# Recurrent attention and a two-layer network on one core: eight chunks of load buffers, later stores, two more chunks turned by DMA

## The chip, the core and the metric

The kernel runs on one core of one Trainium2 chip. A core has five engines with instruction streams of their own: TensorE (PE, matrix products), VectorE (DVE), ScalarE (ACT), GpSimd (POOL) and SyncE (SP). Data moves between main memory and on-chip memory on 16 DMA engines; here SP issues loads and DMA transposes, and POOL issues most stores. The metric is the device time of one execution in microseconds (us), the median of three runs.

## The reference

Four sequences of 768 steps, with 8 heads of 48 numbers, go through a linear recurrence with a decay (step 1). The result, 3072 rows of 384 numbers, goes through two matrix products with a squared relu between them (step 2).

```python
# q, k, v, alpha: (4, 8, 768, 48); alpha lies between 0.8 and 1
for t in range(768):
    state = alpha[:, :, t, :, None] * state + einsum('bhd,bhe->bhde', k[:, :, t], v[:, :, t])
    y[:, :, t] = einsum('bhd,bhde->bhe', q[:, :, t], state)
x = y.transpose(0, 2, 1, 3).reshape(3072, 384)
out = (maximum(x @ w_in, 0) ** 2) @ w_out        # w_in 384x2048, w_out 2048x384
```

## The kernel before

**Chunks.** The 3072 rows are 24 chunks of 128 steps, six to a sequence. Chunks 0 to 3 are handled as two double chunks (`add_super`); chunks 4 to 23 one by one (`add_chunk`), with the scores and what follows them in pairs from chunk 8 on.

**Step 1 in one chunk.** The four inputs of a chunk are loaded by SP (`add_load`, line 362; 192 KB each) into buffers that hold two chunks each, three per input, so six chunks. ACT takes the logarithm of alpha (L431); PE sums it over the steps with a triangle of ones; ACT makes A and its inverse (L459, L463) by exponentials; DVE multiplies q by A (L490, from chunk 12 on) and k by the inverse (L493). POOL casts v (L436). From chunk 12 on A's last row, the chunk's total decay, is sent to where it is needed by two small DMAs that POOL issues (`e_aed`, L476). Then q and k are turned, eight blocks of 128x128, so that heads and features lie on the partitions: up to chunk 17 by PE transposes (the helper at L269) and a DVE copy out of PSUM (L390), from chunk 18 on (`XFROM`) by one DMA transpose that SP issues (`e_turn`, L507). PE forms the scores, DVE masks them (L561), PE multiplies them by v, and adds q times the state; the state is updated by PE, scaled by DVE (L595) and cast by ACT (L600). ACT casts the result (`xn`, L388), and three blocks of it are turned into `xT_big` (`add_tail`): by PE and a DVE copy (L390) up to chunk 17, by a DMA transpose from SP (`e_xturn`, L409) from chunk 18 on.

**Step 2.** `add_moe1` multiplies `xT_big` by w_in in groups of chunks (4, 1, 1, and then pairs), ACT takes the relu (L866) and DVE squares it into `gT` (L874). `add_moe2` multiplies `gT` by w_out chunk by chunk in four quarters. ACT or DVE copies the result to an output tile `ob` (L938, L936), and it is stored: by POOL up to chunk 20 (L947, and L950 for chunks 0 to 3, in halves), by SP for the last three. The weights come through four staging buffers (`stage`) that SP loads (L311) and POOL or ACT casts (L315, L319).

**The order of the work** is planned before it is written out. Each piece of work is an `Op` with an engine or a choice of engines, a duration, what it depends on, a priority and, for PSUM, the banks that it may take. `Plan.run` plays these through: it gives each engine the ready piece that can start first, and writes the instructions out by their planned starts. So every engine has a fixed order, in which an instruction whose input is late holds all behind it. The planned durations are constants in the code; transfers have a time on an engine called "DMA" and a delay until they land. Loads are planned strictly in order. "XB" stands for DMA transposes, `ISSUE` for the time that SP needs for one issue (planned from `ISSUE_AT` us on), `AE_LAT` for the delay of the two small DMAs, `XLAT` for that of a transpose. Stores on POOL are planned not before `OUT_AT + 3.0 * s` us. A function `gate` holds back the logarithm's sum on PE of chunk s until step 2 has come far enough: `LEAD` (3.5) chunks behind, growing to 5 for the later ones. These constants only set the order of the instructions; what an instruction waits for on the chip is its data and its buffer.

Before step 2's second product begins, idle products on a tile of zeros (`warm`) fill the gaps that the plan expects on PE.

Of the kernel before, what the change touches and what calls it, by code (L numbers as in the profile page):

```python
# [8 lines left out]
FP32 = mybir.dt.float32  # L9
# [24 lines left out]
LAT = {"PE": 0.13, "ACT": 0.14, "DVE": 0.13, "POOL": 0.25}  # L34
PE_SLACK = 0.05
ISSUE = {"DMA": 0.6, "OUT": 0.6, "SPD": 1.2, "XB": 1.25}
ISSUE_AT = 75.0
PE_CALM = 25.0
PAUSES = [(13.0, 1.0), (18.0, 1.0)]


# [21 lines left out]
class Plan:  # L63
# [14 lines left out]
    def ready(self, op):  # L78
        t = op.at
        slack = PE_SLACK if "PE" in op.durs else 0.0  # L80
        if slack and self.free.get("PE", 0.0) > PE_CALM:
            slack = 0.25
        for d, x in op.deps:
            if d.done is None:
                return None
            if x is None:
                t = max(t, d.done + (slack if d.eng != "PE" else 0.0))
            else:
                t = max(t, d.start + d.dur + x)
        if op.takes is not None:  # L90
            best = None
            for sl in op.takes:
                f = sl.free_at()
                if f is not None and (best is None or f < best):
                    best, op.slot = f, sl
            if best is None:
                return None
            t = max(t, best)
        return t

    def run(self, gate):
        free = self.free
        while any(self.pending.values()):
            best = None
            for eng, ops in self.pending.items():
                t0 = free.get(eng, 0.0)
                pick = None
                fifo = eng in ("DMA",)
                for op in (ops[:1] if fifo else ops):
                    if not gate(op):  # L110
                        continue
                    r = self.ready(op)
                    if r is None:
                        continue
                    if len(op.durs) > 1:
                        ends = {e: max(r, free.get(e, 0.0)) + x + LAT[e] for e, x in op.durs.items()}
                        if ends[eng] > min(ends.values()):
                            continue
                    key = (max(r, t0), op.prio)
                    if pick is None or key < pick[0]:  # L120
                        pick = (key, op)
                if pick is not None and (best is None or pick[0][0] < best[0]):
                    best = (pick[0][0], eng, pick[1])
            assert best is not None, "nothing can run"
            t, eng, op = best
            for e in op.durs:
                self.pending[e].remove(op)
            op.eng, op.dur = eng, op.durs[eng]
            op.start = t + getattr(op, "late", 0.0)
            if eng == "DMA" and self.pauses and t >= self.pauses[0][0]:  # L130
                op.dur += self.pauses.pop(0)[1]
            free[eng] = t + op.dur
            if op.lat is None:
                op.lat = LAT.get(eng, 0.2)
            if hasattr(op, "hold"):
                free["DMA"] = max(free.get("DMA", 0.0), t) + op.hold
            if hasattr(op, "dma"):
                free["DMA"] = max(free.get("DMA", 0.0), t) + op.dma
            if eng == "OUT":
                free["DMA"] = max(free.get("DMA", 0.0), t) + op.dur  # L140
            op.done = t + op.dur + op.lat
            if eng in ISSUE and t >= ISSUE_AT:
                sp = max(free.get("SPQ", 0.0), t)
                free["SPQ"] = sp + ISSUE[eng]
                op.start = max(op.start, sp)
                op.done = max(op.done, sp + ISSUE[eng] + op.lat)
                if eng == "DMA":
                    free[eng] = sp + op.dur
                    op.done = sp + op.dur + op.lat
            if op.takes is not None:  # L150
                self.ready(op)
                op.slot.release.append(op.gives if op.gives is not None else op)
            self.order.append(op)
            self.on_pick(op)
        self.order.sort(key=lambda o: o.start)
# [3 lines left out]
def kernel(  # L159
# [10 lines left out]
    nc = tc.nc  # L170
# [21 lines left out]

    consts = ctx.enter_context(tc.tile_pool(name="consts", bufs=1))
    big = ctx.enter_context(tc.tile_pool(name="big", bufs=1))
    LB = 6
    loads = ctx.enter_context(tc.tile_pool(name="loads", bufs=LB // 2))
    work = ctx.enter_context(tc.tile_pool(name="work", bufs=4))
    rpool = ctx.enter_context(tc.tile_pool(name="rpool", bufs=8))
    opool = ctx.enter_context(tc.tile_pool(name="opool", bufs=9))
    stage = ctx.enter_context(tc.tile_pool(name="stage", bufs=4))  # L200

    ps_sc = ctx.enter_context(tc.tile_pool(name="ps_sc", bufs=1, space=PSUM))
# [43 lines left out]

    NBUF = 4
    TURN = 12
    AE_LAT = 3.0
    L_s = big.tile([P, NBUF, H, DP], BF16)  # L250
    nc.gpsimd.memset(L_s[:, :, :, D:], 0.0)
    qk_s = big.tile([P, NBUF, 2, H, DP], BF16)
# [4 lines left out]
    nc.gpsimd.memset(kI_s[:, :, :, D:], 0.0)  # L257
    ae_s = big.tile([P, NBUF, 2, NP], FP32)
    nc.vector.memset(ae_s, 0.0)
    xT_big = big.tile([P, KT, n_tok], BF16)  # L260

    def pin(ins):
        tc.keep_in_program_order(ins)
# [75 lines left out]
    SRC = dict(srcs)  # L339
    EARLY = 2 * 3  # L340
    PAIRS = 8
    XFROM, XTO = 18, NT
    XLAT = 2.8
    LEAD = 3.5

    NS = 2
# [6 lines left out]
    def add_load(s, nm):  # L353
        d = C[s]
        b, c = divmod(s, NCH)
        k = s // 2

        def ld():
            if s % 2 == 0:
                PAIR[k][nm] = loads.tile([P, 2, H, D], FP32, name=nm)  # L360
            d[nm] = PAIR[k][nm][:, s % 2]
            pin(nc.sync.dma_start(out=d[nm], in_=SRC[nm][b, c]))
        prev = C[s - LB]["use_" + nm] if s - LB >= 2 * NS else None
        if 2 * NS <= s < 2 * NS + LB and (k - LB // 2) < NS:
            prev = SUP[k - LB // 2]["use_" + nm]
        pace = C[s - LB + 1]["use_" + nm] if s >= TURN + 2 else None
        d["ld_" + nm] = add("DMA", LD if s < TURN else 0.97, ld, prev, pace, lat=2.4)

    PAIR = [dict() for _ in range(NT // 2)]
    SRC2 = [("at", alpha), ("qt", q), ("kt", k), ("vt", v)]  # L370
# [23 lines left out]
    def add_tail(s, done, first, g):  # L394
        d = C[s]

        def e_xn():
            d["xn"] = work.tile([P, HD], BF16, name="xn")
            cast(xn, d["xn"], d["py"][:, 0:HD])
        xn = add("ACT", 0.36, e_xn, done, **g)  # L400
        first.gives = xn

        def e_p4():
            d["px"] = psum(p4, [P, KT, P], BF16)
            for j in range(KT):
                tr(d["px"][:, j, :], d["xn"][:, j * P:(j + 1) * P], ident_bf)
        if XFROM <= s < XTO:
            def e_xturn():
                pin(nc.sync.dma_start_transpose(out=xT_big[:, :, s * P:(s + 1) * P], in_=d["xn"]))  # L409
            d["x"] = add("XB", 0.0, e_xturn, xn, lat=XLAT - 0.9)  # L410
            d["end"] = xn
            return
        p4 = plan.add(Op("PE", 0.165, e_p4, [xn], takes=GLA_BANKS, lat=0.14, **g))

        def e_xT():
            cast(xT, xT_big[:, :, s * P:(s + 1) * P], d["px"])
        xT = add({"ACT": 0.36, "DVE": 0.27} if s < EARLY else "DVE", 0.27, e_xT, p4, prio=-9.0)
        d["x"] = d["end"] = xT
        p4.gives = xT

    def add_chunk(s):
# [55 lines left out]
        if s < TURN:  # L477
            ae0 = add("ACT", 0.18, e_ae0, p0, after(ai), **g)
            p0.gives = ae1 = add("ACT", 0.19, e_ae1, p0, after(ae0), **g)
        else:  # L480
            p0.gives = ai
            ae1 = add("POOL", 1.8, e_aed, a_, lat=AE_LAT, prio=-20.0)
            ae1.dma = 0.3

        def e_qA():
# [33 lines left out]
        elif s < XFROM:  # L519
            cp = cpk = add("DVE", 0.61, lambda: e_cp(0, 2 * NP), p1k, **g)  # L520
        else:
            cp = cpk = add("XB", 0.0, e_turn, mq, mk, lat=XLAT)
        if s < XFROM:
            p1q.gives = cpk

# [305 lines left out]
    NGT = 3  # L831
    FIRST = sl_bank[4:1:-1]
    M2_LAST = sl_bank[::-1]
    OUT_AT = 72.0
    LAST_COLS = ((0, 256), (256, 384))
    RELU_PRIO = -20.0
    RELU_PRIO0 = 0.0
    DUMMY = 1
    COLD = 8.0
    sq = {}  # L840
    prog = {"m1": 0.0, "m2": 0.0}

    def add_moe1(g, f0, before, lo=0, hi=None, per=1):
        hi = GN[g] if hi is None else hi
        t0, n = (GT[g] + lo) * P, (hi - lo) * P
        w = per * n
        box = {}
        op = before
# [62 lines left out]
    def add_moe2(g, tt, before, box, quarters, pools):  # L911
# [17 lines left out]
            before = op  # L929
        if quarters[-1] < NQ - 1:  # L930
            return op

        def e_ev():
            box["ob"] = opool.tile([P, d_model], FP32, name="ob")
            if ev.eng == "DVE":
                pin(nc.vector.tensor_copy(box["ob"], box["po"]))  # L936
            else:
# [1 line left out]
        ev = add({"DVE": 0.47, "ACT": 0.38}, 0, e_ev, op, prio=-15.0)  # L939
        box["first"].gives = ev  # L940

        s = GT[g] + tt
        q = nc.gpsimd if s < NT - 3 else nc.sync

        def e_out():
# [3 lines left out]
                for t in range(2):  # L949
                    pin(q.dma_start(out=out2_r[s, t], in_=box["ob"][HF * t:HF * t + HF]))  # L950
        if s < NT - 3:
            add("POOL", 1.0, e_out, ev, at=OUT_AT + 3.0 * s, lat=2.5, prio=5.0).dma = 0.55
        else:
            add("OUT", 0.55, e_out, ev)
        return op
# [37 lines left out]
    def gate(op):  # L993
        s = getattr(op, "gla", None)
        if s is not None:
            return s <= (LEAD if s < 12 else min(5.0, LEAD + 0.25 * (s - 11))) + (prog["m1"] + prog["m2"]) / 5.12
        return True

    def on_pick(op):
# [54 lines left out]
```

## Time and profile before

| what | value |
|---|---|
| median of three runs | 181.93 us (181.58 to 182.31) |
| profiled execution, its own time | 181.87 us |
| its span | 180.1 us |
| instructions | 4934 |
| PE, weight loads, DVE, ACT, POOL busy | 174.0, 129.4, 130.3, 122.4, 54.2 us |
| granted TensorE clock | 1.00 |
| read from main memory, written to it | 25.17 MB, 4.72 MB |

The span runs from the first to the last instruction in the trace; the execution's own time has some 1.8 us around it. Matrix products are pipelined and their ends are modelled, so that a mean duration of one (268 ns) is longer than the distance between two. Lines 266 and 269 are helpers that issue all products and all PE transposes. DMA shares are means over the 16 engines, and can be a little over 1. "A <- B" in a wait means that A's engine stood until B was done.

### The profile page before, as it was taken

The numbers are of one execution on the slowest core, as the hardware profiler recorded it, in microseconds if no ns is written. First come the engines' busy times: TensorE is split into PE (matmuls) and PEld (weight loads), VectorE is DVE, ScalarE is ACT, GpSimd is POOL, SyncE is SP. The second block draws the span as 40 slices with busy tenths as digits, with TensorE's granted clock in tenths as the row PEclk, the third lists the DMA queues.
The fourth block names the chain that finished last, engine by engine and source line by source line (L and its number), as shares of the span: only waits on it lengthen the run. The fifth ranks groups of instructions, "written<-read, shape, count | busy, mean of one in ns | idle before, by whom it ended". The sixth has DMA issues, their size and how long they took to land.

```text
span 180.1 us, 4934 instructions
## 1 busy us (share of the span) xinstructions
PE 174.0 (97%) x1926; PEld 129.4 (72%) x1927; DVE 130.3 (72%) x269; ACT 122.4 (68%) x260; POOL 54.2 (30%) x95
## 2 busy tenths in 40 slices
PE   7799999999999999999999999999999999999993
PEld 3467684566996788866877887878767866868663
DVE  6699669847799889885999897997864971724300
ACT  4556879357997598937685967889577863657421
POOL 6023466612111116503643504543245022011100
PEclk9999999999999999999999999999999999999999
DMA  5999999999998989989999694596276325031022
GB/s 141 274 277 321 323 356 378 214 211 215 189 202 166 224 172 232 289 185 214 198 273 278 151 223 109 132 195 155 54 106 155 77 44 146 5 87 44 4 87 87
DMA packets 107799, 32.39 MB, mean 180 GB/s; under 512 B 101840, under 2 KB 106064, under 8 KB 107776
## 3 DMA queue, kind: packets, MB, share of 16 engines
q1 hardware_dynamic: 105536, 27.93, 70.3%
q0 software_dynamic: 2240, 4.15, 6.5%
q8 instruction: 15, 0.25, 0.6%
q14 instruction: 8, 0.07, 0.1%
HBM read 25.17 MB, written 4.72 MB: 166 GB/s over the span
## 4 chain that ended last, share of the span: by engine, by line
PE 87%; DVE 4%; ACT 3%; DMA 2%; issue 2%; SPq 1%; ACTq 0%; DVEq 0%
PE bank L266 77%; PE bank L269 5%; DMA at<-in_alpha_dram 2%; PE sc L266 2%; PE st L266 2%; ACT r L866 2%; DVE qkT L390 1%; DVE sm L753 1%; SPq L383 1%; DVE qk_s L690 1%; ACT xn L388 0%; DVE xT_big L390 0%; DVE qk_s L487 0%; ACT L_s L638 0%; ACT A L674 0%
## 5 line engine op out<-in xcount | busy, mean ns | idle before, releaser
L266 PE MATMUL bank<-xT_big,w_in_b 128*128 128x256 bf16 (+2 forms) x599 | 72.5, 268 | 0.2
L266 PE MATMUL bank<-w_out_b,gT 128*128 128x384 bf16 (+2 forms) x400 | 70.4, 319 | 0.0
L866 ACT ACTIVATE r<-bank 128x512 bf16<-128x512 f32 x96 | 56.8, 607 | 12.6 <-PE bank L266 10.4
L266 PEld LDWEIGHTS <-w_in_b 128*128 128x128 bf16 x600 | 52.9, 98 | 9.9 <-issue 0.3
L874 DVE TENSOR_TENSOR gT<-r 128x512 bf16<-128x512 bf16 x96 | 45.0, 500 | 13.4 <-ACT r L866 13.1
L266 PEld LDWEIGHTS <-gT 128*128 128x128 bf16 x400 | 36.9, 98 | 19.0
L436 POOL CAST vb<-vt 128x384 bf16<-128x384 f32 x20 | 12.0, 607 | 44.4 <-DMA vt<-in_v_dram 19.3
L938 ACT COPY ob<-bank 128x384 f32<-128x384 f32 x19 | 9.1, 481 | 17.6 <-PE bank L266 17.5
L947 POOL DMA_DIRECT2D out_dram<-ob x17 | 9.4, 555 | 33.1 <-ACT ob L938 31.2
L476 POOL DMA_DIRECT2D ae_s<-Af x24 | 12.2, 509 | 20.7 <-ACT Af L459 20.4
L561 DVE TENSOR_TENSOR sm<-sc,utri_b 128x512 bf16<-128x512 f32 x24 | 15.4, 687 | 2.8 <-PE sc L266 2.8
L388 ACT CAST xn<-bank 128x384 bf16<-128x384 f32 x24 | 11.2, 486 | 5.8 <-PE bank L266 5.6
L390 DVE COPY qkT<-bank 128x1024 bf16<-128x1024 bf16 (+1 forms) x20 | 12.4, 634 | 3.1 <-PE bank L269 2.9
L269 PE MATMUL bank<-ident_bf,qk_s 128*128 128x128 bf16 x144 | 13.0, 219 | 1.2 <-DVE qk_s L690 1.0
L266 PEld LDWEIGHTS <-qkT 64*128 64x128 bf16 (+2 forms) x304 | 10.5, 97 | 5.0 <-issue 2.2
L490 DVE TENSOR_TENSOR qk_s<-qt,Af 128x384 bf16<-128x384 f32 x12 | 10.3, 862 | 5.0 <-ACT Af L459 4.9
L269 PEld LDWEIGHTS <-qk_s 128*128 128x128 bf16 x144 | 9.7, 98 | 4.0 <-DVE qk_s L690 1.5
L459 ACT ACTIVATE Af<-bank 128x384 f32<-128x384 f32 x12 | 10.5, 873 | 2.2 <-issue 1.2
L493 DVE TENSOR_TENSOR qk_s<-kt,Ainv 128x384 bf16<-128x384 f32 x20 | 11.7, 587 | 0.1
L431 ACT ACTIVATE L_s<-at 128x384 bf16<-128x384 f32 x20 | 10.3, 527 | 1.5 <-DMA at<-in_alpha_dram 1.5
L595 DVE TENSOR_TENSOR st<-st,ae_s 128x384 f32<-128x384 f32 x16 | 9.0, 561 | 2.1 <-ACT xn L388 1.8
L463 ACT ACTIVATE Ainv<-bank 128x384 bf16<-128x384 f32 x20 | 10.3, 517 | 0.0
(71 smaller groups left out, 172.6 us busy)
## 6 DMA issues: line engine op xcount, KB each, us to landing
at<-in_alpha_dram SPq DMA_DIRECT2D x24, 192.0 KB, 4.0
qt<-in_q_dram SPq DMA_DIRECT2D x24, 192.0 KB, 4.1
kt<-in_k_dram SPq DMA_DIRECT2D x24, 192.0 KB, 4.1
vt<-in_v_dram SPq DMA_DIRECT2D x20, 192.0 KB, 3.9
out_dram<-ob POOLq DMA_DIRECT2D x17, 192.0 KB, 2.3
wo<-in_moe_w_out_dram SPq DMA_DIRECT2D x4, 768.0 KB, 7.4
wi<-in_moe_w_in_dram SPq DMA_DIRECT2D x4, 384.0 KB, 6.5
wi<-in_moe_w_in_dram SPq DMA_DIRECT2D x2, 768.0 KB, 5.2
```

The source lines that it names most:

```text
L266: pin(nc.tensor.matmul(*a, **kw))
L269: pin(nc.tensor.transpose(*a))
L388: pin(nc.scalar.copy(out_t, in_t))
L390: pin(nc.vector.tensor_copy(out_t, in_t))
L431: pin(nc.scalar.activation(L[:, :, 0:D], d["at"], AF.Ln))
L436: pin(nc.gpsimd.tensor_copy(d["vb"], d["vt"]))
L459: pin(nc.scalar.activation(d["A"], split(d["pm"][:, 0:HD], s), AF.Exp))
L476: pin(nc.gpsimd.dma_start(out=ae_s[HF * j:HF * j + D, i, j], in_=d["Af"][P - 1:P, j]))
L493: pin(nc.vector.tensor_mul(kI[:, :, 0:D], d["kt"], d["Ai"]))
L561: pin(nc.vector.tensor_mul(d["sm"][:, hh], d["sc"][hh], utri_b.to_broadcast([P, NP, P])))
L866: pin(nc.scalar.activation(box["r"][:, 0:w], box["ph"][:, 0:w], AF.Relu))
L874: pin(nc.vector.tensor_mul(gT[g][:, f0:f0 + per, lo * P:lo * P + n], r, r))
```

## The change

- The load buffers hold eight chunks instead of six (`LB`).
- `xT_big` holds ten chunks instead of all 24; chunk s uses place s mod 10 (`XR`).
- The output tiles are no longer taken from a pool of nine, but from the four staging buffers of the weights: one buffer holds the results of four chunks (`held`). The pool of output tiles keeps two, for the last chunk.
- Stores on POOL are planned from `104 + 2.5 * s` us on instead of `72 + 3.0 * s`, with 0.56 us of POOL's time instead of 1.0.
- DMA transposes are used from chunk 16 on instead of 18.
- In the plan: a DMA transpose is issued at least 2.0 us behind its input (`XB_SLACK`), takes 0.9 or 0.4 us of the DMA engines' planned time, and has a shorter delay; the two small DMAs take 1.03 us of POOL instead of 1.8 and land 2.0 us later instead of 3.0; SP's issue time is planned from 50 us on instead of 75; a load takes 0.95 us instead of 0.97 from chunk 12 on; the gate grows to 6 chunks instead of 5.

```diff
-ISSUE_AT = 75.0
+ISSUE_AT = 50.0
 PE_CALM = 25.0
+XB_SLACK = 2.0
...
             slack = 0.25
+        if "XB" in op.durs:
+            slack = XB_SLACK
...
                 op.done = max(op.done, sp + ISSUE[eng] + op.lat)
+                if eng == "XB":
+                    free["DMA"] = max(free["DMA"], sp) + op.turn
+                    op.done = max(op.done, free["DMA"] + op.lat)
...
-    LB = 6
+    LB = 8
+    XR = 10
...
-    opool = ctx.enter_context(tc.tile_pool(name="opool", bufs=9))
+    opool = ctx.enter_context(tc.tile_pool(name="opool", bufs=2))
...
-    AE_LAT = 3.0
+    AE_LAT = 2.0
...
-    xT_big = big.tile([P, KT, n_tok], BF16)
+    xT_big = big.tile([P, KT, XR * P], BF16)
...
-    XFROM, XTO = 18, NT
-    XLAT = 2.8
+    XFROM, XTO = 16, NT
+    XLAT = 2.2
...
-        d["ld_" + nm] = add("DMA", LD if s < TURN else 0.97, ld, prev, pace, lat=2.4)
+        d["ld_" + nm] = add("DMA", LD if s < 12 else 0.95, ld, prev, pace, lat=2.4)
...
-                pin(nc.sync.dma_start_transpose(out=xT_big[:, :, s * P:(s + 1) * P], in_=d["xn"]))
-            d["x"] = add("XB", 0.0, e_xturn, xn, lat=XLAT - 0.9)
+                pin(nc.sync.dma_start_transpose(out=xT_big[:, :, s % XR * P:(s % XR + 1) * P], in_=d["xn"]))
+            d["x"] = add("XB", 0.0, e_xturn, xn, lat=XLAT - 0.8)
+            d["x"].turn = 0.4
...
-            cast(xT, xT_big[:, :, s * P:(s + 1) * P], d["px"])
+            cast(xT, xT_big[:, :, s % XR * P:(s % XR + 1) * P], d["px"])
...
-            ae1 = add("POOL", 1.8, e_aed, a_, lat=AE_LAT, prio=-20.0)
+            ae1 = add("POOL", 1.03, e_aed, a_, lat=AE_LAT, prio=-20.0)
...
             cp = cpk = add("XB", 0.0, e_turn, mq, mk, lat=XLAT)
+            cp.turn = 0.9
...
-    OUT_AT = 72.0
+    OUT_AT = 104.0
...
+    held = {}
...
-        t0, n = (GT[g] + lo) * P, (hi - lo) * P
+        t0, n = (GT[g] + lo) % XR * P, (hi - lo) * P
...
         def e_ev():
-            box["ob"] = opool.tile([P, d_model], FP32, name="ob")
+            if s % 4 == 0:
+                held[s // 4] = stage.tile([P, 4, d_model], FP32, name="held", tag="stage")
+            box["ob"] = held[s // 4][:, s % 4]
...
-            add("POOL", 1.0, e_out, ev, at=OUT_AT + 3.0 * s, lat=2.5, prio=5.0).dma = 0.55
+            add("POOL", 0.56, e_out, ev, at=OUT_AT + 2.5 * s, lat=2.5, prio=5.0).dma = 0.55
...
-            return s <= (LEAD if s < 12 else min(5.0, LEAD + 0.25 * (s - 11))) + (prog["m1"] + prog["m2"]) / 5.12
+            return s <= (LEAD if s < 12 else min(6.0, LEAD + 0.25 * (s - 11))) + (prog["m1"] + prog["m2"]) / 5.12
```

More of the change, by code (lines that the diff above doesn't have):

```diff
@@ L931, in add_moe2 @@
             return op
+        s = GT[g] + tt
         def e_ev():
-            box["ob"] = opool.tile([P, d_model], FP32, name="ob")
+            if s % 4 == 0:
+                held[s // 4] = stage.tile([P, 4, d_model], FP32, name="held", tag="stage")
+            box["ob"] = held[s // 4][:, s % 4]
             if ev.eng == "DVE":
@@ L940, in add_moe2 @@
         box["first"].gives = ev
-        s = GT[g] + tt
         q = nc.gpsimd if s < NT - 3 else nc.sync
```

## The prediction

> **What bounds the kernel now.** I read the page's first two parts, then stretches of 15 us, the waits of TensorE (PE), the chain of waits, the groups by line, and SyncE's (SP's) queue. Busy times and the forty slices of the span:
>
> ```profile
> PE 174.0 (97%) x1926; PEld 129.4 (72%) x1927; DVE 130.3 (72%) x269; ACT 122.4 (68%) x260; POOL 54.2 (30%) x95
> ...
> PE   7799999999999999999999999999999999999993
> ...
> DMA  5999999999998989989999694596276325031022
> ```
>
> PE is full from the third slice to the last but one; the DMA engines are full for some 24 slices (to about 108 us) and have room after that. The stretches (busy us of PE, weight loads, DVE, ACT, POOL; then granted clock, DMA share, GB/s):
>
> ```profile
> 25.00:40.00 15.00, 14.95 (x99) 8.97 (x99) 12.07 (x17) 9.93 (x20) 7.63 (x6) 1.00 1.05 284
> 40.00:55.00 15.00, 14.88 (x244) 12.18 (x241) 12.49 (x26) 12.67 (x32) 2.25 (x4) 1.00 1.04 205
> 55.00:70.00 15.00, 14.87 (x188) 11.52 (x181) 13.02 (x28) 11.95 (x31) 2.30 (x5) 1.00 0.96 190
> ...
> 85.00:100.00 15.00, 15.00 (x170) 11.94 (x169) 13.65 (x28) 10.81 (x23) 6.68 (x14) 1.00 1.09 244
> 100.00:115.00 15.00, 15.00 (x172) 12.06 (x171) 13.84 (x28) 12.18 (x26) 6.90 (x13) 1.00 0.66 143
> 115.00:130.00 15.00, 15.00 (x171) 11.84 (x169) 13.07 (x30) 11.92 (x23) 4.52 (x8) 1.00 0.69 145
> ```
>
> From 25 to 70 us PE misses 0.30 us of 45; from 70 to 175 us nothing, at a clock of 1.00, and its list of waits after 70 us is empty. So nothing that comes sooner (a load, a store, a buffer) can shorten those 105 us; only less work for PE can. The chain of waits (start, us, what), in which line 269 is PE's transposing:
>
> ```profile
> PE 87%; DVE 4%; ACT 3%; DMA 2%; issue 2%; SPq 1%; ACTq 0%; DVEq 0%
> ...
> 103.23 0.22 PE bank L269 x4
> ...
> 104.11 0.22 PE bank L269 x4
> ...
> 113.59 0.22 PE bank L269 x4
> ...
> 114.14 0.22 PE bank L269 x4
> ...
> 120.61 0.34 PE bank L269 x6
> ...
> 153.45 23.94 PE bank L266 x214
> ```
>
> By the times of the multiplies before them, the first two pieces turn chunk 16's q and k, the next two chunk 17's, and the six at 120.61 turn both chunks' results.
>
> **The change part by part.** The sum is against the profiled execution, 181.87 us (span 180.1, 1.8 around it); the median of the runs is 181.93.
>
> *Turning from chunk 16 on.* PE loses 2 x 8 + 2 x 3 = 22 transposes. In the chain they take 4 x 0.22 + 0.34 = 1.22 us, 55 ns each. The groups give another price:
>
> ```profile
> L269 PE MATMUL bank<-ident_bf,qk_s 128*128 128x128 bf16 x144 | 13.0, 219 | 1.2 <-DVE qk_s L690 1.0
> L390 DVE COPY xT_big<-bank 128x384 bf16<-128x384 bf16 x13 | 4.5, 356 | 3.9 <-PE bank L269 3.9
> ...
> qkT<-qk_s SPq DMA_TRANSPOSE x6, 3.4
> xT_big<-xn SPq DMA_TRANSPOSE x6, 2.3
> ```
>
> 13.0 us over 144 is 90 ns, or 1.99 us for 22; but that busy time includes the overlap at a group's ends. I take 1.22, since it is PE's own pace in the full stretch, and keep 1.99 as the far end. All of it is on the path. DVE loses two copies of 0.69 and two of 0.36, 2.1 us, in stretches where it is 13.07 to 13.84 busy of 15; no PE wait hangs on them, so zero, but room.
>
> In return come four DMA turnings. SP issues one in 1.2 to 1.3 us, so 5 us more of its queue. The way to the scores gets longer: for chunk 17 the k multiply ends at 113.63 and the scores start at 115.60, 1.97 us; for chunk 19, already turned by DMA, 124.24 to 129.04, 4.80 us. The way from the results to the first product gets longer too: 1.24 us for 16 and 17 (last cast ends 120.30, copy ends 121.54), 2.4 us for 18 and 19 (133.77 to 133.9 + 2.3 = 136.2). Together 4.0 us later. What covers it: when the first product of chunks 16 and 17 starts at 122.24, the second product of chunks 13, 14 and 15 is still to come (they start at 127.6, 131.1 and 134.6), 16 x 162 ns = 2.6 us each, 7.8 us of PE work whose inputs are made. So zero; without cover, up to 4.0 us. After it, the pairs follow as 18/19 does now, which cost PE no gap.
>
> *SP's order.* Planned issues of turnings now lie at least 2 us behind their inputs. Behind a turning that waits, SP holds loads. Now it is loads that hold it:
>
> ```profile
> 96.59 0.67 SPq L362 DMA_DIRECT2D at<-in_alpha_dram  x1
> 100.58 0.37 SPq L362 DMA_DIRECT2D qt<-in_q_dram  x1
> ...
> 106.38 1.08 SPq L362 DMA_DIRECT2D at<-in_alpha_dram  x1
> 113.19 0.37 SPq L362 DMA_DIRECT2D qt<-in_q_dram  x1
> ...
> 115.87 1.34 SPq L507 DMA_TRANSPOSE qkT<-qk_s  x1
> ```
>
> Chunk 20's q waits until 100.58 for the multiply of chunk 15, chunk 22's until 113.19 for that of chunk 17. With a fourth pair of buffers chunk 20 waits for chunk 13 (done 86.4), chunk 22 for chunk 15 (100.6). The last load, issued at 120.3 now, then comes at about 100.6 + 8 x 1.0 = 108.6. Chunk 16's q and k, multiplied by 103.7, are turned among those last loads (4.1 us to landing instead of 3.4), but they are needed only with chunk 17's, at 115.6 or later: hidden. Chunk 17's come when the loads are out.
>
> *Stores.* Ten chunks' stores leave before 104 us now; they will leave after it, one per 2.5 us planned. The software queue moved 4.15 MB in 6.5% of the span, 11.7 us, so a store is 0.56 us of all DMA engines: 5.6 us are taken out of the full stretch and put where the share is 0.15 to 0.69. The loads gain, PE does not: zero. The last three chunks' stores stay on SP, so the end (PE ends at 177.4, the span at 180.1) is as before: zero. The buffers that hold the results are the weights' (last cast ended 35.0, first result 37.6); their first reuse, by chunk 16 (147.5 now), needs the stores of chunks 0 to 3, planned to be out by 111.5: zero.
>
> *Tighter plan.* A chunk's total decay (A's last row), sent by DMA, is planned at 1.03 + 2.0 us instead of 1.8 + 3.0. The trace has 1.02 for the two issues and 1.5, 1.8 and 4.8 to landing (least, median, most), the 4.8 between 82 and 104 us beside loads and stores. If late, DVE's state update waits first, then the state's cast on ACT, then PE's next product with the state. DVE's update shows no such wait now. I take zero; the bound is the 4.8 less the planned 2.0, 2.8 us, if PE stood for all of it. The deeper gate (6 chunks instead of 5) lets later chunks do their gated work up to one chunk sooner; it moves work, and adds none. The ring of ten for xT makes chunk 16's turning wait for the first product of chunk 6, begun at 62: zero. Up to some 50 us the plan should order work as now.
>
> Sum: 181.87 - 1.22 = 180.65 us.
>
> One rule speaks against the change. The Trainium skill (VectorE: DVE Perf Modes, section "The three transpose paths", and its rules for authors) gives 390 ns for a 128x128 turning on TensorE and 1309 ns by DMA, and advises TensorE wherever PSUM will do as the target. By these figures PE would be freed of 22 x 0.39 = 8.6 us, an estimate, and eight blocks one behind another would take 10.5 us to land. The trace agrees with neither: 0.22 us for four on PE, 3.4 us for the eight by DMA, so measurement decides.
>
> **The rivals.** *(1) Turned too late (slower).* Place: scores or first product of chunks 16 and 17. If the new order has used up the second products of chunks 13 to 15 before the turned results land, PE stands for up to the 4.0 us, and ends at 180.65 + 4.0 = 184.7. It decides from 2.1 us uncovered (1.22 and half a per cent). For it: PE's order is fixed in advance, and these same 7.8 us now cover pair 18/19. Against: that pair leaves no gap. The skill's serial figure for DMA would be this case too. *(2) Gain given back (same).* The plan is rerun, and everything after 50 us may change place; before 70 us such orders cost PE 0.30 us in 45, and a late decay up to 2.8. Some 0.4 to 2 us of new gaps give 181.0 to 182.7. Also in it: DVE, which has 40.56 us of work in the 45 from 85 to 130, less 2.1, plus up to one chunk's 3.4 (0.86 + 0.59 + 2 x 0.69 + 0.56) through the deeper gate, 41.9: tight, but room. *(3) More than forecast.* The groups' 1.99 us and the old 0.30 us of gaps: 179.6. *(4) Doesn't do what it says:* the loads may end late still, if SP is blocked elsewhere; PE does not care, so the time is the forecast's.
>
> **How the numbers follow.** Half a per cent, 0.9 us (about what can be told from no change), puts the bounds at 181.0 and 182.8. Forecast, 179.9 to 181.0, with (4): 0.56. More (3): 0.04. Same (2): 0.18. Slower (1), 182.8 to 184.7: 0.22. So faster 0.60, same 0.18, slower 0.22. The range goes from 179.8 to 183.4, which leaves out about a tenth above, mostly (1)'s end, and a few hundredths below; the likeliest case alone has 179.9 to 181.0. The point is 180.7: 1.22 less than the median as well as the profiled run, rounded.
>
> **What would show it.** Right: eight turnings each of qkT and xT in the DMA list; 22 fewer transposes on PE and about 1.2 us less chain in line 269; PE at 15.00 in every stretch from 70 us; no store before 100 us; the last load issued near 108. Wrong: PE waits for xT, qkT or a cast of the state between 105 and 135 us, a stretch of PE under 14.5, or a first product of chunks 16 and 17 that starts late with no second product before it.

## The result and the profile after

The changed kernel takes 183.35 us (median of six, 182.11 to 184.09), the kernel before 181.8 us beside it; the ratio is 1.008 (95% interval 1.0058 to 1.0103). Ratios, here and below, are of mean times, without the three executions (one of f4, two of g1) that ran over 1.5% longer than the fastest of their kernel; medians are of all. The forecast was 180.7, so it is wrong in sign; the time lies at the upper end of the range. The profiled execution took 184.09 us, the highest of the six. A second profile of the same kernel (run f1 below) took 183.03, so both are used.

First the work itself: the page's busy times, the slices of PE and of the DMA engines, and lines of the list of groups (busy us, mean ns, idle before) and of DMA issues (median us to landing) of the kernel after:

```profile
PE 174.8 (96%) x1905; PEld 128.6 (71%) x1905; DVE 126.5 (69%) x264; ACT 122.2 (67%) x261; POOL 53.2 (29%) x95
PE   7899899999999999999999999989999999999993
DMA  5999889999989999899999999996547633101122
L276 PE MATMUL bank<-ident_bf,qk_s 128*128 128x128 bf16 x128 | 11.4, 224 | 0.7 <-DVE qk_s L699 0.5
ae_s<-Af POOLq DMA_DIRECT2D x24, 0.8 KB, 3.1
qkT<-qk_s SPq DMA_TRANSPOSE x8, 4.1
xT_big<-xn SPq DMA_TRANSPOSE x8, 2.5
```

The change did what it says. Chunks 16 and 17 are turned by DMA (eight turnings of each kind, 16 of the turns of q and k gone from PE). But a turning takes 4.1 us to land instead of 3.4, and the decay rows `ae_s` take 3.1 us instead of 1.8. The DMA engines, which had room from about 108 us, are now full to about 123.

Where PE lost shows in the stretches of 15 us (busy us of PE, weight loads, DVE, ACT, POOL; granted clock, DMA share, GB/s):

```profile
85.00:100.00 15.00, 14.95 (x165) 11.71 (x163) 14.50 (x29) 11.62 (x24) 5.56 (x11) 1.00 1.00 195
100.00:115.00 15.00, 14.57 (x158) 11.18 (x156) 12.63 (x27) 12.24 (x25) 7.77 (x16) 1.00 1.01 205
115.00:130.00 15.00, 14.22 (x146) 9.71 (x145) 11.29 (x22) 8.74 (x18) 6.76 (x13) 1.00 0.96 211
130.00:145.00 15.00, 14.98 (x165) 12.10 (x163) 11.71 (x25) 13.56 (x28) 6.75 (x13) 1.00 0.58 135
```

Before, each of these four had 15.00 us of PE; now 0.43 us are missing from 100 to 115 us and 0.78 from 115 to 130. The list of waits from 98 to 125 us (us in total, times, longest) has one line in which PE's products wait, and on DVE one that names a late transfer:

```profile
PE bank L273 <- DVE sm L570: 1.1, 2, 0.8
DVE st L604 <- DMA ae_s<-Af: 0.7, 1, 0.7
```

PE stands for the masks that DVE makes (`sm`, L570), not for a turned tile, a load or a cast of the state. The chain of waits (start, us, what) shows why the mask is late the second time:

```profile
117.75 0.06 DVE st L604
...
118.23 0.85 DVE qk_s L498
119.08 0.34 DVE gT L884
119.41 0.47 DVE qk_s L501
119.88 0.67 DVE gT L884 x2
120.55 0.87 DVE sm L570 x2
...
122.40 0.53 PE bank L273 x12
```

From 117.75 to 122.40 us the end of the kernel hangs on DVE's queue, and that queue began with a state update `st` (L604). The timeline (start, us, then the idle time before it and what ended it) has the two updates that DVE stood for, the small DMA of the second, and the two products of PE that then came late:

```profile
101.37 0.57 DVE L604 TENSOR_TENSOR st<-st,ae_s 128x384 f32<-128x384 f32 x1 [0.67 <-DMA ae_s<-Af]
...
106.28 0.33 PE L273 MATMUL bank<-sb,qkT 128*128 128x96 bf16 x4 [0.36 <-DVE sm L570]
...
113.33 1.01 POOL L484 DMA_DIRECT2D ae_s<-Af  x2 [0.20 <-issue]
...
117.75 0.57 DVE L604 TENSOR_TENSOR st<-st,ae_s 128x384 f32<-128x384 f32 x1 [1.19 <-PE bank L273]
...
122.40 0.33 PE L273 MATMUL bank<-sb,qkT 128*128 128x96 bf16 x4 [0.78 <-DVE sm L570]
```

The label of the wait at 117.75 ("PE bank L273") is not the cause: the last PE product on that state tile (st, 116.38) ended 1.03 us before the update began. What remains is the decay row, issued 113.33 to 114.34. The trace has the landing of each issue: the second of these, begun at 113.83 us, took 3.80 us and was there at 117.63, 0.12 us before the update began. The row of the first late update landed at 101.25, again 0.12 us before it. The plan had 113.33 + 1.03 + 2.0 = 116.4 for the second. All rows issued between 104 and 120 us took 3.2 to 4.0 us (before, 1.6 to 2.9). From the update at 101.37 to the masks that end at 106.82 DVE's timeline shows no idle time, so the first delay reaches PE through that queue too.

**Balance.** I count from the first second product on PE to PE's last product: 145.55 us before, 146.49 in this profile and 146.46 in f1. PE has 22 transposes less there (154 before, 132 now), 1.22 us at 55 ns. So the new standing is worth 146.49 - 145.55 + 1.22 = 2.16 us (f1: 2.13): more than the change saved, a loss of 0.94 us. The rows give most of it. A bracket of PE understates a stand by about 0.17 us, since the modelled end of the last product lies so far behind its pace (12 products of 162 ns are 1.94 us, the row has 2.11). At 106 us 0.36 + 0.17 and a smaller 0.2 behind the second mask, at 122 us 0.78 + 0.17: 1.7 us, behind the two late updates. By the distances between the starts of products there are shorter stands of 0.2 us at 93.1 (a mask), 0.18 at 133.1 and 0.13 at 136.7, where ACT is busy 13.56 us of 15: some 2.2 us in all. The two profiled executions differ by 2.22 us, and the rest of that is not from there. 0.99 us is a later start of the second product (32.83 instead of 31.84 us), behind a late load of v. It did not come again in f1 (31.85), but did in f3 below (32.76), so it comes and goes from execution to execution. The last 0.27 us lie behind PE's end: the span goes on for 3.02 us, before for 2.75. The last store lands 1.86 us after PE's end (before, 1.85), so it is not that; the longer end shows in every run below that turns chunk 16 by DMA (3.00 to 3.15 us) and in no other (2.75 to 2.79).

### The profile page after: what moved, and what is told of

It is laid out like the page before. It is cut to its first block, busy times and chain, and to the rows that moved or that the text cites. A ratio compares the mean times of both kernels' runs of the same rounds, so it can differ in the third digit from the quotient of the medians.

```text
span 182.3 us, 4884 instructions
## 1 busy us (share of the span) xinstructions
PE 174.8 (96%) x1905; PEld 128.6 (71%) x1905; DVE 126.5 (69%) x264; ACT 122.2 (67%) x261; POOL 53.2 (29%) x95
## 4 chain that ended last, share of the span: by engine, by line
PE 79%; DVE 7%; DMA 6%; SPq 5%; issue 1%; POOL 1%; ACT 0%; DVEq 0%
PE bank L273 70%; SPq L390 5%; PE bank L276 4%; DVE sm L570 4%; DMA vt<-in_v_dram 4%; PE sc L273 2%; PE st L273 2%; DMA qt<-in_q_dram 2%; DVE gT L884 1%; POOL vb L655 1%; DVE qk_s L501 1%; DVE qk_s L498 0%; DVE xT_big L397 0%; SPq L318 0%; DVE qk_s L495 0%
## 5 line engine op out<-in xcount | busy, mean ns | idle before, releaser
L273 PE MATMUL bank<-xT_big,w_in_b 128*128 128x256 bf16 (+2 forms) x600 | 71.8, 268 | 0.1
L273 PE MATMUL bank<-w_out_b,gT 128*128 128x384 bf16 (+2 forms) x400 | 69.5, 319 | 0.0
L273 PEld LDWEIGHTS <-w_in_b 128*128 128x128 bf16 x600 | 53.0, 98 | 9.7 <-issue 0.5
L884 DVE TENSOR_TENSOR gT<-r 128x512 bf16<-128x512 bf16 x96 | 43.6, 478 | 12.8 <-ACT r L876 12.3
L273 PEld LDWEIGHTS <-gT 128*128 128x128 bf16 x400 | 37.0, 98 | 20.1
L444 POOL CAST vb<-vt 128x384 bf16<-128x384 f32 x20 | 11.0, 551 | 53.1 <-DMA vt<-in_v_dram 24.6
L951 ACT COPY held<-bank 128x384 f32<-128x384 f32 x20 | 9.6, 480 | 20.9 <-PE bank L273 20.1
L570 DVE TENSOR_TENSOR sm<-sc,utri_b 128x512 bf16<-128x512 f32 x24 | 15.4, 686 | 2.4 <-PE sc L273 2.3
L959 POOL DMA_DIRECT2D out_dram<-held x17 | 9.3, 550 | 26.7 <-ACT held L951 26.7
L273 PEld LDWEIGHTS <-qkT 64*128 64x128 bf16 (+2 forms) x304 | 10.5, 97 | 6.6 <-issue 4.2
L397 DVE COPY qkT<-bank 128x1024 bf16<-128x1024 bf16 (+1 forms) x18 | 11.1, 629 | 3.4 <-PE bank L276 3.4
L276 PE MATMUL bank<-ident_bf,qk_s 128*128 128x128 bf16 x128 | 11.4, 224 | 0.7 <-DVE qk_s L699 0.5
L604 DVE TENSOR_TENSOR st<-st,ae_s 128x384 f32<-128x384 f32 x16 | 9.0, 561 | 3.3 <-PE st L273 1.4
L276 PEld LDWEIGHTS <-qk_s 128*128 128x128 bf16 x128 | 8.6, 100 | 3.5 <-issue 1.3
```

Of the source, the lines that this page charges most:

```text
L273: pin(nc.tensor.matmul(*a, **kw))
L276: pin(nc.tensor.transpose(*a))
L397: pin(nc.vector.tensor_copy(out_t, in_t))
L444: pin(nc.gpsimd.tensor_copy(d["vb"], d["vt"]))
L570: pin(nc.vector.tensor_mul(d["sm"][:, hh], d["sc"][hh], utri_b.to_broadcast([P, NP, P])))
L884: pin(nc.vector.tensor_mul(gT[g][:, f0:f0 + per, lo * P:lo * P + n], r, r))
```

## The experiments

Ratios are to the kernel before on the same chip, with their 95% intervals. "PE" is the time from the first second product to PE's end in the one profile of each; the new standing in it is that less 145.55, plus 1.22 where chunks 16 and 17 are fully turned by DMA.

| run | kernel it starts from, and the edit | median us | ratio | PE, us |
|---|---|---|---|---|
| f1 | changed, none | 183.76 | 1.0106 (1.0066 to 1.0146) | 146.46 |
| e1 | changed, decay rows planned as before | 182.48 | 1.0023 (0.9996 to 1.0050) | 146.03 |
| e2 | changed, turning from 18 as before | 183.80 | 1.0083 (1.0053 to 1.0112) | 147.86 |
| e3 | before, the tighter decay plan alone | 183.70 | 1.0073 (1.0046 to 1.0101) | 147.32 |
| e4 | before, turning from 16 alone | 184.03 | 1.0130 (1.0087 to 1.0172) | 147.12 |
| f2 | before, a load planned at 0.96 us, not 0.97 | 182.10 | 1.0003 (0.9985 to 1.0022) | 145.34 |
| f3 | e1, stores as early as before | 183.63 | 1.0067 (1.0034 to 1.0100) | 146.14 |
| f4 | e1, v's cast planned behind k's multiply | 182.44 | 1.0036 (1.0006 to 1.0066) | 145.34 |
| g1 | e1, results of 16 and 17 turned by PE | 183.06 | 1.0051 (1.0030 to 1.0072) | 145.70 |
| g2 | g1 and f4 | 186.48 | 1.0237 (1.0193 to 1.0281) | 149.50 |
| g3 | changed, landing of the decay rows planned at 3.8 us | 182.67 | 1.0032 (1.0007 to 1.0057) | 146.07 |
| g4 | e1, gate 5 as before | 182.85 | 1.0048 (1.0027 to 1.0069) | 145.78 |
| h1 | e1, stores from 118 us | 182.55 | 1.0025 (1.0006 to 1.0044) | 145.82 |
| h2 | g3, stores from 118 us | 182.28 | 1.0009 (0.9991 to 1.0028) | 146.54 |
| h3 | e1, a turning planned at 4.0 us | 183.54 | 1.0094 (1.0066 to 1.0123) | 146.78 |
| h4 | h3, stores from 118 us | 184.12 | 1.0108 (1.0090 to 1.0126) | 147.33 |
| i1 | h1, v's casts of 18, 19 planned behind k's multiply of 17 | 182.16 | 0.9995 (0.9976 to 1.0014) | 145.63 |
| i2 | h2, the same | 182.34 | 0.9998 (0.9977 to 1.0020) | 145.56 |

**The theory after the result** was that the tighter plan for the decay rows costs the most. The rivals were that turning from chunk 16 on costs it (too late a turning), and that any rerun of the plan loses the full stretch of PE.

**e1 and e3: the decay plan undone, and alone.**

```diff
-    AE_LAT = 2.0
+    AE_LAT = 3.0
...
-            ae1 = add("POOL", 1.03, e_aed, a_, lat=AE_LAT, prio=-20.0)
+            ae1 = add("POOL", 1.8, e_aed, a_, lat=AE_LAT, prio=-20.0)
```

e3 makes the opposite edit to the kernel before.

> The changed kernel, with the decay rows planned as before (1.8 us of POOL and 3.0 us until they land, instead of 1.03 and 2.0). Theory D (the rows land later than planned, 3.1 us by the median and up to some 4 us; DVE's state update waits for them, the masks of the scores queue behind it, PE stands): no gap of PE over 0.3 us is left between 90 and 125 us, and the time falls by the gaps of the changed kernel's profile there, about 2 us, to 0.997 to 1.002 of the kernel before. Rival T (DMA turnings that hold loads in SP's queue, and come late themselves): the plan of the decay rows does not matter, and the ratio stays near 1.008. Rival S (the first 25 us are slower by 1.0 us because buffers lie elsewhere): PE's second product starts at 32.8 us again, not at 31.8, and at least 1.0 us of the loss stays.

> The kernel before, with only the plan of the decay rows tightened to 1.03 and 2.0 us. Theory D: PE gets gaps of 0.5 to 2.5 us between 85 and 115 us, where the transfers are full; ratio 1.003 to 1.013. Rival T: no change, 0.998 to 1.002.

Undone, the kernel takes 182.48 us, and its interval (to 1.0050) does not reach those of the changed kernel (from 1.0058 and 1.0066): some 0.6 to 0.8% are due to this edit. DVE stands nowhere for a decay row. The PE column moves less, from 146.49 to 146.03 us, since e1 has two new stands of PE, at 112 and 120 us (below); the expectation of no gap over 0.3 us was missed. Alone, the edit makes the kernel before 0.7% slower, in the same way. In e3's timeline of DVE:

```profile
89.92 0.57 DVE L595 TENSOR_TENSOR st<-st,ae_s 128x384 f32<-128x384 f32 x1 [0.89 <-DMA ae_s<-Af]
...
91.53 1.28 DVE L561 TENSOR_TENSOR sm<-sc,utri_b 128x512 bf16<-128x512 f32 x2
92.73 1.28 DVE L561 TENSOR_TENSOR sm<-bank,utri_b 128x512 bf16<-128x512 f32 x2
```

and in its list of waits from 85 to 100 us:

```profile
DVE st L595 <- DMA ae_s<-Af: 0.9, 1, 0.9
ACT sb L600 <- DVE st L595: 0.6, 1, 0.6
PE bank L266 <- DVE sm L561: 0.4, 1, 0.4
PEld L266 <- ACT sb L600: 0.4, 1, 0.4
```

PE is busy 14.22 us of 15 in that stretch, and 15.00 in the kernel before. A row that is 0.89 us late on DVE has become 0.78 us on PE (some 1.3 by the distances between starts, of the 1.77 in the PE column), by way of the mask and, here, of the state's cast (`sb`) too. The decay theory holds, from both sides.

**e2 and e4: turning from 16 undone, and alone.**

```diff
-    XFROM, XTO = 16, NT
+    XFROM, XTO = 18, NT
```

e4 makes the opposite edit to the kernel before.

> The changed kernel, but DMA turning begins with chunk 18, as before. Theory D: the decay rows are planned as tightly as in the changed kernel, so PE has gaps of 1 to 2 us between 90 and 125 us, and the 1.2 us of transposes come back as well: ratio 1.010 to 1.018. Rival T: the gaps go, the transposes come back: ratio 0.998 to 1.004. Rival S: second product at 32.8 us in either case.

> The kernel before, with only the DMA turning begun at chunk 16. Theory D: the 22 transposes taken off PE pay in full, no new gap: 1.2 us less, ratio 0.992 to 0.995. Rival T: the turnings wait in SP's queue among loads that wait for their buffers (six chunks), and hold them; PE waits for the results of chunks 16 and 17: ratio 1.003 or more.

Alone it is the dearest part, 1.3%. The list of waits of e4 from 100 to 145 us and its queue of SP:

```profile
PE bank L266 <- DMA xT_big<-xn: 2.1, 1, 2.1
PE bank L266 <- DVE xT_big L390: 0.5, 1, 0.5
```

```profile
120.96 2.51 SPq L409 DMA_TRANSPOSE xT_big<-xn  x1
123.57 0.53 SPq L362 DMA_DIRECT2D vt<-in_v_dram  x1
124.19 1.25 SPq L409 DMA_TRANSPOSE xT_big<-xn  x1
```

Chunk 17's result waits in SP's queue behind the turning of 16 and a load, and PE stands 2.1 us: this is rival (1) of the prediction, but only without the change's other parts. The 0.5 us, at 112, are behind a k multiply of 1.58 us beside two of POOL's casts, which comes again in e1 below. In e2 those parts stay and the turning is taken away, and the time stays where the changed kernel's is (1.0083, below the 1.010 to 1.018 expected). DVE stands for a decay row there too, 1.31 us at 101.39. Its profile says that turning from 16 is worth 147.86 - 146.49 = 1.37 us there, close to the 1.22 predicted; the medians (183.80 against 183.35 and 183.76) do not show it. That difference stays open.

**f1 and f2: the changed kernel again, and a rerun of the plan that changes next to nothing.**

```diff
-        d["ld_" + nm] = add("DMA", LD if s < TURN else 0.97, ld, prev, pace, lat=2.4)
+        d["ld_" + nm] = add("DMA", LD if s < TURN else 0.96, ld, prev, pace, lat=2.4)
```

> The changed kernel as it is, on the chip of the next three. Theory D: DVE stands again for decay rows, 1 to 2 us in all beyond its other inputs, near 101 and 118 us; ratio 1.006 to 1.010. Where PE's second product starts (32.8 us in the first profile, 31.7 to 32.2 in four others) shows whether that one late microsecond belongs to the change: Rival S says 32.8 again, chance says 31.7 to 32.3.

> The kernel before, with a load planned at 0.96 us instead of 0.97 from chunk 12 on: a hundredth of a microsecond that changes no dependence, only the order that comes out (PE's order differs in some hundred rows). Theory P (any new order loses the fit of the old one: casts on POOL then meet multiplies on DVE, inputs come late by chance): PE loses 0.5 to 2 us between 70 and 145 us, ratio 1.003 to 1.010. Theory D alone: 0.998 to 1.002.

f1 confirms the loss and both DVE waits (0.93 us at 100.9, 0.49 beyond the other inputs at 116.7). In f2 PE has 15.00 us in every stretch of 15 from 70 to 145. So this rerun of the plan costs nothing, and a rerun need not lose the full stretch. One rerun does not show that none does: g4, h3 and h4 below have stands of 0.3 to 0.75 us, for ACT or a mask, that come with their own order. The waits for decay rows are not of that kind: from 85 to 125 us DVE stands over 0.2 us for one in all four profiles with the tighter plan (the changed kernel's two, e2, e3) and in none without it.

**g3: leave POOL's 1.03 us, plan the landing as it is.** The edit is `AE_LAT = 3.8` in the changed kernel.

> The changed kernel with the decay rows planned at 1.03 us of POOL, as measured, and 3.8 us until they land, near the most of the trace (4.2) instead of 2.0. Theory D: what counts is the sum until landing (4.83 us, as the 4.8 of before), so DVE stands for no decay row over 0.2 us and the ratio is that of e1, 1.000 to 1.005. If the planned time on POOL was what mattered: DVE stands again, ratio 1.006 to 1.010.

No wait for a decay row is left, and the ratio falls to 1.0032. So it was the planned landing that was wrong, not POOL's 1.03 us. But its list of waits has something new, 0.9 us of PE for a turned tile (`qkT`).

**f3, f4, g1, g4: what is left in e1.** e1 still has 146.03 - 145.55 + 1.22 = 1.70 us of new standing. Its waits from 98 to 125 us, and DVE and POOL around the first:

```profile
PE bank L273 <- DVE xT_big L397: 0.6, 1, 0.6
PE bank L273 <- DMA qkT<-qk_s: 0.3, 1, 0.3
```

```profile
110.20 1.59 DVE L501 TENSOR_TENSOR qk_s<-kt,Ainv 128x384 bf16<-128x384 f32 x1
110.42 0.96 POOL L444 CAST vb<-vt 128x384 bf16<-128x384 f32 x2
111.72 0.34 DVE L397 COPY xT_big<-bank 128x384 bf16<-128x384 bf16 x1
112.11 1.14 PE L273 MATMUL bank<-xT_big,w_in_b 128*128 128x256 bf16 x9 [0.55 <-DVE xT_big L397]
```

The k multiply of chunk 17 takes 1.59 us instead of 0.55 while POOL casts v; the copy behind it, and PE, wait. With 0.17 added to each bracket, this is 0.7 us, the turned tile 0.5, and short stands from 137 to 142 us some 0.4. The edits, each on e1: `OUT_AT = 72.0` with `3.0 * s` (f3); a dependence of the cast on its own chunk's multiply (f4); 18 in place of `XFROM` in the turning of results (g1); `min(5.0, ...)` in the gate (g4).

```diff
+        if s >= TURN:
+            vb.deps.append((mk, None))
...
-        if XFROM <= s < XTO:
+        if 18 <= s < XTO:
```

> The changed kernel with the decay rows planned as before, and the stores as early as before (72 us and 3.0 us a chunk) instead of from 104 us. If the later stores keep the DMA engines full from 100 to 130 us (share 1.07 to 1.09 in e1, 0.66 to 0.69 before): share 0.75 to 0.95 there, decay rows land in 2 to 2.6 us instead of 3.0 by the median, ratio 0.996 to 1.001. If it is the turnings among the loads that keep them full: share over 1.0, ratio 1.002 as in e1.

> The changed kernel with the decay rows planned as before, and POOL's cast of v made to wait for DVE's multiply of k in the same chunk, from chunk 12 on. In e1 two such casts lay in one multiply of k, which took 1.59 us instead of 0.55, and PE then stood 0.71 us for the copy behind it. If that meeting is the cause: no multiply of k over 0.9 us from chunk 12 on, no gap of PE at 111 us, ratio 0.995 to 1.000. If the long multiply is chance or another cause: it is there again, ratio 1.002.

> As e1 (decay rows planned as before), but the results of chunks 16 and 17 are turned by PE, as before; only their q and k are turned by DMA. PE saves 16 transposes, 0.88 us, instead of 1.22. If the late results of 16 and 17 (first product begun at 130.3 us in e1, 122.4 before) and the pile of first products after them (ACT busy 13.6 of 15 us from 130 to 145) cost the rest in e1: first product at 122 to 126, excess of PE between 115 and 145 us below 0.2 us instead of 0.7, ratio 0.995 to 1.000. If not: ratio 1.002 to 1.005.

> As e1, with the gate grown to 5 chunks, as before, instead of 6. If the deeper gate crowds DVE and ACT between 115 and 145 us: excess of PE there falls from 0.7 us, ratio 0.996 to 1.000. If the gate does not matter: ratio 1.002 as in e1.

Early stores bring nothing back (1.0067), so the later stores are not shown to cost anything, and my expectation for f3 was missed. In f4 the multiply meets one cast instead of two and takes 1.22 us (0.9 at most was expected), and the new standing sinks to 145.34 - 145.55 + 1.22 = 1.01 us, but its median is that of e1. With the results of 16 and 17 turned by PE (g1) PE has 15.00 us from 115 to 130, but the gap at 111 us stays and the time is not better. The gate is not the cause: with 5 the stand at 111 us is still there and one of 0.75 us at 139 is added. The interval of each of the four overlaps e1's.

**g2: both together.**

> As g1, and POOL's cast of v waits for the multiply of k as in f4. If both costs are real and add: no gap of PE over 0.35 us from 70 us on, ratio 0.993 to 0.998. If the two orders disturb each other: as g1 or slower.

It fails by its own order. SP's queue from 113 us, and PE's wait:

```profile
113.21 2.06 SPq L515 DMA_TRANSPOSE qkT<-qk_s  x1
...
116.42 2.30 SPq L515 DMA_TRANSPOSE qkT<-qk_s  x1
...
120.75 4.84 SPq L515 DMA_TRANSPOSE qkT<-qk_s  x1
```

```profile
PE bank L273 <- DMA qkT<-qk_s: 2.2, 1, 2.2
```

A turning holds SP for 2 us and more here, and PE stands 2.2 us from 126 on. It says nothing on the v casts.

**h1 to h4: stores still later, turnings planned longer.** `OUT_AT = 118.0` on e1 (h1), on g3 (h2); `XLAT = 4.0` on e1 (h3), and both (h4).

> As e1 (decay rows planned as before), and the stores held back 14 us longer, to 118 us, past the turnings of chunks 16 to 18. In e1 these turnings land 5.1 to 6.5 us after their issue (3.3 before, without loads and stores beside them), and PE stood 0.34 us for one. If the stores from 103 us on are what delays them: landing 3.5 to 5 us, no wait of PE for a turned tile, ratio 0.996 to 1.001. If the loads alone delay them: landing 5 us or more, ratio as in e1, 1.002.

> As g3 (decay rows planned at 1.03 us and 3.8 us until they land), with the stores held back to 118 us. PE stood 0.9 us for a turned tile in g3. If stores delay it: no such wait, ratio 0.995 to 1.001; if loads alone: 0.5 us or more of that wait again, ratio 1.003.

> As e1, with a turning planned to land 4.0 us behind its issue instead of 2.2, as late as the trace shows it among loads. If lateness against the plan is what costs: PE waits for no turned tile; the scores of chunks 16 and 17 and the first product come 2 us later still; ratio 0.997 to 1.002. If the later first product piles up more work behind it: excess of PE from 130 to 145 us over 0.4 us, ratio 1.002 to 1.006.

> As h3, with the stores held back to 118 us. If both causes count and add: ratio 0.994 to 1.000, the best of all. If one of the two is empty: the same as the better of h1 and h3.

With the stores after 118 us q and k land 4.4 us (median) behind their issue between 104 and 124 us, in e1 6.1, and no PE wait for a turned tile is left, nor is one in h2: stores do delay turnings. In time it is worth less than can be told here (1.0025 against 1.0023, 1.0009 against 1.0032). Planning the turnings at about what they take (h3, h4) makes it worse, by 0.7 to 0.8%, more than either expectation had: PE then stands 0.57 us (h3) between 135 and 140 us, for ACT, and in h4 0.7 us for a mask.

**i1 and i2: move the casts away.**

```diff
+        if s in (18, 19):
+            vb.deps.append((C[17]["mk"], None))
```

> As h1 (decay rows planned as before, stores from 118 us), and POOL's casts of v for chunks 18 and 19 wait for DVE's multiply of k in chunk 17, beside which they lay in e1, g1, g4 and h1 to h4 (that multiply took 1.57 to 1.60 us each time, instead of 0.55, and PE stood 0.5 us for the copy behind it). If the two engines shut each other out there: the multiply takes 0.55 to 0.6 us, the 0.7 us gap at 111 us goes, ratio 0.997 to 1.000, a version no slower than either. If the long multiply has another cause: it stays, ratio 1.0025.

> As h2 (decay rows planned at 1.03 and 3.8 us, stores from 118 us), with the same two casts moved. If the meeting is the cause: no multiply of k over 0.9 us between 100 and 130 us, no gap of PE over 0.3 us there, ratio 0.995 to 0.999. If not: 1.001 as h2.

These equal the kernel before (0.9995 and 0.9998), and no version beats it. The intervals of i1 and h1, and of i2 and h2, overlap, so a gain of the edit is not shown. The edit did not do what it was for. In i1:

```profile
110.63 1.57 DVE L501 TENSOR_TENSOR qk_s<-kt,Ainv 128x384 bf16<-128x384 f32 x1
110.82 0.96 POOL L444 CAST vb<-vt 128x384 bf16<-128x384 f32 x2
```

The dependence moves the cast in the plan only. The cast and the multiply share no data, so nothing on the chip keeps POOL behind DVE, and they met again. Whether the whole gap at 111 us can be had by keeping the casts away is open; in f4, with one cast beside the multiply, PE's wait there is 0.2 us instead of 0.6.

## Why the prediction was wrong, point by point

**Tighter plan** is the step that failed. It read the landings correctly (1.5, 1.8 and 4.8 us) and then took zero against a bound of 2.8, because DVE showed no wait in the kernel before. That was evidence for the old plan of 1.8 + 3.0 us; the new one, 1.03 + 2.0, takes 1.8 us of its room away. Measured: two DVE waits, 0.67 and 1.03 us (f1 0.93 and 0.49), and 1.7 us of PE behind them in the changed kernel, 0.78 us in e3. The first of the two late rows took 4.1 us, within the 4.8 that the step had read for that stretch; only the second, 3.8 us at 113.8, came where the kernel before had 1.6 to 2.9. Over all rows the median landing grew to 3.1 us. The path was only half right: the step named the cast of the state as next. What stood was all that follows in DVE's queue, and PE stood for the masks.

**Turning from chunk 16 on.** The 1.22 us are right: 22 transposes are gone, and e2's profile is 1.37 us longer without it. The zero for the end of the kernel is not: 0.25 us more behind PE's end come with this part. That the 7.8 us of second products would cover a late turning held: PE does not wait for `xT_big` or `qkT`. But "after it, the pairs follow as 18/19 does now" was wrong. The first product of 16 and 17 started at 130.8 us instead of 122.2, so that step 2's first products came close together, ACT had 13.56 us of work in 15 instead of 11.20, and PE had short stands of 0.13 and 0.18 us there. The cover is also thin: e4, g2 and g3 lose 2.1, 2.2 and 0.9 us to the same two transfers.

**SP's order.** "The last load near 108.6" was wrong: it was issued at 121.29 us (before, 120.30). The free buffers did what the step says: chunk 20's q was issued at 97.25 us instead of 100.58, and chunk 22's at 107.65 instead of 113.19. What came behind was held, since turnings and loads alternate in SP's queue:

```profile
97.25 2.09 SPq L369 DMA_DIRECT2D qt<-in_q_dram  x1
...
104.16 2.19 SPq L515 DMA_TRANSPOSE qkT<-qk_s  x1
106.40 0.58 SPq L369 DMA_DIRECT2D vt<-in_v_dram  x1
...
107.65 1.03 SPq L369 DMA_DIRECT2D qt<-in_q_dram  x1
...
111.16 1.42 SPq L515 DMA_TRANSPOSE qkT<-qk_s  x1
112.68 0.83 SPq L369 DMA_DIRECT2D vt<-in_v_dram  x1
```

With turning from 18 (e2) the last load goes out at 114.31 us, with the stores after 118 us (h1) at 115.93. So the turnings were not moved out of the loads' way, as the step had it; loads, turnings, stores and decay rows all met between 100 and 125 us. It is likely that this is why the decay rows of that stretch got later (3.2 to 4.0 us instead of 1.6 to 2.9), and two runs separate it in part. Without the turnings of 16 and 17 (e2) rows issued there still take 3.2 to 3.7 us, so these are not needed for it; with the stores after 118 us (h1) they take 2.6 to 2.9, in e1 2.8 to 4.4, so the stores have a share in it.

**Stores.** "The loads gain, PE does not" is right, but the loads gained little. With 0.99 MB of stores gone from 85 to 100 us SP's queue moves 2.86 MB instead of 2.61, and the engines in all 195 GB/s at a share of 1.00 instead of 244 at 1.09. h1 and h2 show that stores matter to turnings, but little to the time.

**The rivals.** Rival (2), gain given back, is the one that happened, through the mechanism it named (a late decay, with a bound of 2.8 us). Its price was put at 0.4 to 2 us; 2.16 was measured, and so it ended as slower and not as same. Rivals (1), (3) and (4) did not occur as cases of the changed kernel, though half of (4) is true: the loads ended late. That the range still held 183.35 us is luck: its upper part was there for the end of rival (1), which did not happen.

**Open.** The balance of the two profiles gives 0.94 us on PE and 0.26 behind its end. The medians lose 1.55 and 1.75 us. What the remaining 0.35 to 0.55 us are, and why e2's median hides the 1.37 us of its profile, was not settled; the late start of the second product, which comes and goes, may be a part of it. Of e1's 1.70 us of new standing the trace names the waits, but no run that removed one of them was faster than e1 by more than the intervals allow for. Some of the kernels that turn from chunk 16 on also scatter more (f1 183.0 to 185.4 us, f4 181.8 to 184.5), others do not (i1 181.9 to 182.5); the long executions were not profiled.

## What to carry to other kernels

An in-order plan with slack for a transfer shows no wait for it, and that is no proof that the slack is unneeded: price a shorter planned latency by the planned landing against the measured one in the stretch where it will run, and count what stands behind the waiting instruction in its engine's queue, not only its data's path. When a change fills a stretch of DMA that was empty, every small transfer in that stretch has to be priced anew. A dependence that exists only in a planner orders two engines on paper and not on the chip.

## What was not expected of the hardware

A GpSimd cast stops a VectorE multiply entirely. The k multiply takes 0.55 us alone; beside two casts of 0.96 us together it takes 1.57 to 1.60 us in all eleven profiles where that happens, about the sum of both, and it ends some 0.4 us after the second cast (e1: casts to 111.38, multiply to 111.79; i1: 111.78 and 112.20). Beside one cast of 0.5 us it takes 1.08 to 1.26 us. The Trainium skill (SBUF — State Buffer, section "SBUF: two separate sides") says that a VectorE instruction with two inputs in SBUF contends with a GpSimd instruction that reads SBUF, and that the one that starts first holds the port for its whole length while the other fully blocks. The full block agrees with the trace. The order does not show in the records: the multiply's record starts 0.2 us before the first cast's (spans on GpSimd are rough), and it is still the multiply that waits.

After a stand of 2.2 us the TensorE clock fell once. In g2 PE stands until 128.47 us; by stretches of 2 us (columns as above):

```profile
126.00:128.00 2.00, 0.31 (x8) 0.13 (x7) 1.29 (x2) 0.30 (x1) 0.00 (x0) 1.00 0.90 92
128.00:130.00 2.00, 1.53 (x19) 1.29 (x20) 1.10 (x2) 0.28 (x1) 0.00 (x0) 0.97 0.00 0
130.00:132.00 2.00, 2.00 (x9) 1.14 (x8) 1.04 (x3) 0.92 (x2) 0.00 (x0) 0.50 0.00 0
132.00:134.00 2.00, 2.00 (x29) 1.62 (x27) 0.00 (x0) 0.96 (x2) 0.00 (x0) 0.68 0.00 0
```

A mean of 0.97 from 128 to 130 us means that the clock falls to 0.50 shortly before 130, some 1.4 us after the stand has ended, and PE loses about 0.5 x 2 + 0.32 x 2 = 1.6 us more. In e4 a stand of 2.1 us left it at 1.00, so that the stand is the cause is not shown. The Trainium skill (TensorE: Matmul & The Clock Gate, section "HAM oscillation — how this bites in real kernels") puts the abstract rule at idle gaps over about 3.4 us; here the clock fell once after a shorter one.
